# Expert stage of an attention, mixture and dense kernel: place of one weight split per expert, and the queue of the row loads

## The chip, the cores and the metric

One core of a Trainium2 chip runs the whole kernel. The metric is the device time of one execution in microseconds; it is the median of several runs.

## What is computed

Three stages follow each other, each fed by the one before: attention within clusters, a mixture of 8 experts, and a dense network with 2048 hidden columns. The change lies in the mixture. Its reference:

```python
e_idx = np.argmax(x @ w_gate, axis=1)
for e in range(E):                      # E = 8, x is 1536 x 512
    mask = e_idx == e
    h = np.maximum(x[mask] @ w1[e], 0.0)        # w1[e]: 512 x 1024
    ye = h @ w2[e]                              # w2[e]: 1024 x 512
    out[mask] = gate_w[mask, None] * eom[mask, e, None] * ye
```

The products are made in fp32 precision out of two rounded parts each: a value is split into a high part (rounded by a cast) and a low part (the value less the high part), and the product sums high x high, high x low and low x high.

## The kernel before, in words

The routing stage sorts the token rows by expert into a buffer in memory (`xd`) and writes a small table (`plan`) that says which expert comes first (experts are worked off by falling number of rows, with 320, 272, 240, 224, 208, 192, 176 and 160 columns, the table `CAPS`) and where its rows lie. Below, expert 0 is the one that is worked off first, expert 7 the last.

The expert stage is one loop (L1054 to L1088) over groups g = 8e + c, eight for an expert (c0 to c7), each over 128 of the 1024 hidden columns. The program is written in the order in which every engine is to work (a manual schedule), so the order of the emitted lines is each engine's order. One group emits:

- `split_pair` of the weight half that is needed three groups later: ACT casts 128x1024 fp32 values from the buffer `raw` to the high half (L750), and the low half is a subtraction (L753), on POOL in three groups of four, and on DVE, put off to the end of the group, where c is 3 or 7. Then `loads_to` issues the load of the weight half that comes four later into the `raw` buffer that this frees (four buffers, SP's queue, L736). Such an issue waits until the low half has been taken.
- In two or three late groups of an expert, `win_x`: 128 rows of the next expert (`xr`, loaded through `win_load`, L821) are transposed on PE (L834, into `pxt`), and split by ACT (L838) and DVE (L839).
- `win_h`: PE forms the hidden columns (`ph`, L846 to L851). From expert 2 on (at most 256 columns) the two halves of the sum lie side by side in PSUM: ACT copies one (`hs`, L856), DVE adds the other (L857), function `total`. ACT takes relu as the high part (L871, `ht`), and DVE makes the low part (L874), put off to the end of the group.
- `win_y` of the group two earlier: PE adds that group's share to the four sums `py` (L846 to L851). The sums of one expert fill four PSUM buffers, and there is no second set: the next expert's first `win_y` (in its group c2) can start once they have been read.
- In group c1, where the expert before has its last share, `win_out` reads those sums. With at most 256 columns it does so by four `total`s into `room` (ACT L856 and DVE L857 four times); then ACT casts `room` to `yth` (L898), and POOL makes `ytl` (L899), both put off to the end of the group. With more columns (experts 0 and 1, so in group c1 of experts 1 and 2) ACT casts the sums themselves (L902) and DVE makes the low part (L903).
- At the end of the group: the low halves put off, then one step of `dense_step`, which prepares the weights of the dense stage: ACT L784, DVE L785, L788, L791 and L794, ACT L799 and POOL L800, one or two of these in a group.
- In group c0, `win_start(e + 1)` loads the rows of the next expert: one DMA for all of them, into the one `xr` buffer, on SP's queue, behind the weight load of that group.

The register values that such a DMA needs (the expert's place, `exps`) are read from `plan` by SP ahead of the loop.

```python
            if g + 3 < len(order):
                n_, half = order[g + 3]
                split_low = split_pair(ekeys[n_], half, None, nc.vector if g % 4 == 3 else nc.gpsimd, g % 4 == 3)
                loads_to(g + 7)
```

Of the kernel before, what the change touches and what calls it, by code (L numbers as in the profile page):

```python
# [21 lines left out]
NT = B * S  # L22
DM = H * D
E = 8
# [4 lines left out]
CAPS = (320, 272, 240, 224, 208, 192, 176, 160)  # L29
# [6 lines left out]
ACT_E, DVE_E, POOL_E, SP_E = mybir.EngineType.Activation, mybir.EngineType.DVE, mybir.EngineType.Pool, mybir.EngineType.SP  # L36
# [9 lines left out]
def attention_moe_ffn(ctx: ExitStack, tc: tile.TileContext, q, k, v, centroids, w_gate, w_og, w1, w2, w_in, w_out, out):  # L46
    nc = tc.nc
    const = ctx.enter_context(tc.tile_pool(name="const", reuse_waits="tile", bufs=1))

    def f32(ap):  # L50
        return ap.bitcast(F32)
# [37 lines left out]
    xd = dram.tile([E * NT, DM], F32, name="xd")  # L89
# [545 lines left out]
    pieces = {}  # L635
# [8 lines left out]
    with tc.manual_schedule():  # L644
# [14 lines left out]
        for i in range(NS + 2):  # L659
            nu, r = divmod(i + 3, 12)  # L660
# [22 lines left out]
            n = i - (1 if tail else 2)  # L683
# [25 lines left out]
    def need(x, names):  # L709
        for nm in names:  # L710
            tc.add_manual_dep(x, nm, DATA_DEP, reason="all of them scattered")

    def experts(ap):
        return nc.values_load_multi_w_load_instructions(ap, engines=[SP_E], min_val=0, max_val=E - 1)[1]

    exps = list(experts(lead))

    ps_y = ctx.enter_context(tc.tile_pool(name="ps_y", reuse_waits="tile", bufs=1, space=PSUM))
# [9 lines left out]
    def load_half(key, i, ex, pool=None):  # L728
        d = pairs.setdefault(key, {})
        if ex is None:  # L730
            src = pair_of(w_in, w_out, key[2])
        else:
            src = pair_of(w1[bass.ds(ex, 1)].rearrange("o d f -> (o d) f"), w2[bass.ds(ex, 1)].rearrange("o f d -> (o f) d"), key[2])
        t = (pool or raw).tile([128, 1024], F32, name="raw", tag="raw")
        g = src[i].shape[1]
        nc.sync.dma_start(out=t.rearrange("p (g n) -> p g n", g=g), in_=src[i])  # L736
        d["raw", i] = t

    def halves(d, half, pool=None):

        if ("w", half) not in d:
            d["w", half] = (pool or wp).tile([128, 2, 1024], F32R, name=f"w{half}", tag=f"w{half}")
        return d["w", half]

    def split_pair(key, half, pool=None, eng=None, defer=False):
        d = pairs[key]
        w = halves(d, half, pool)
        r = d.pop(("raw", half))
        hi, lo = w[:, 0], w[:, 1]
        nc.scalar.copy(hi, r)  # L750

        def rest():
            (eng or nc.gpsimd).tensor_tensor(lo, r, f32(hi), op=ALU.subtract)  # L753
        if defer:
            return rest
        rest()
# [51 lines left out]
        return pairs[key]["w", 1][:, part].rearrange("p (i d) -> p i d", i=2)[:, i]  # L808


    def win_load(ex_row, n, one_tile=False, pieces=False):
        nr = -(-n // 128)
        if one_tile:
            x = hp.tile([128, 2 * CAP], F32R, name="ht", tag="ht")[:, None, :DM].bitcast(F32)
        else:
            x = xp.tile([128, WR, DM], F32, name="xr", tag="xr", bufs=1)
        d = {"n": n, "nr": nr, "x": x}
        for r0 in range(0, nr, 1 if pieces else nr):
            m, p = (1, min(128, n - r0 * 128)) if pieces else (nr, 128)
            row = nc.s_assert_within(ex_row + r0 * 128, 0, E * NT - 128, skip_runtime_bounds_check_because="inside the rows of an expert") if r0 else ex_row  # L820
            x = nc.sync.dma_start(out=d["x"][:p, r0:r0 + m], in_=xd[bass.ds(row, m * p)].rearrange("(r p) c -> p r c", p=p)).ins  # L821
            need(x, scatters)
        return d

# [28 lines left out]
    def total(ps, n, t):  # L853

        half = hp.tile([128, max(CAPS[2:])], F32, name="hs", tag="hs", bufs=2)[:, :n]
        nc.scalar.copy(half, ps[:, n:2 * n])  # L856
        nc.vector.tensor_tensor(t, ps[:, :n], half, op=ALU.add)  # L857
        return t
# [28 lines left out]
    def win_out(d, col, defer=False):  # L887
        n = d["n"]
        cs = bass.ds(col, n)
        if n > 256:  # L890
            ys = [py[:, :n] for py in d["py"]]
        else:
            room = xp.tile([128, 4 * max(CAPS[2:])], F32, name="room", tag="room", bufs=1)[:, :4 * n].rearrange("p (m n) -> p m n", m=4)
            ys = [total(d["py"][m], n, room[:, m]) for m in range(4)]

        def rest():
            if n <= 256:
                nc.scalar.copy(yth[:, :, cs], room)  # L898
                nc.gpsimd.tensor_tensor(ytl[:, :, cs], room, f32(yth)[:, :, cs], op=ALU.subtract)  # L899
                return  # L900
            for m, y in enumerate(ys):
                nc.scalar.copy(yth[:, m, cs], y)  # L902
                nc.vector.tensor_tensor(ytl[:, m, cs], y, f32(yth)[:, m, cs], op=ALU.subtract)  # L903
        if defer and n <= 256:
            return rest
        rest()
# [3 lines left out]
    ekeys = [("e", e, c) for e in range(E) for c in range(4)]  # L910
# [3 lines left out]
    order = [(0, 0), (1, 0), (0, 1)]  # L914
# [3 lines left out]
    def loads_to(n):  # L918

        while loaded[0] < min(n, len(order)):  # L920
            n_, half = order[loaded[0]]
            load_half(ekeys[n_], half, exps[ekeys[n_][1]], rawd if loaded[0] < 2 else None)
            loaded[0] += 1
# [4 lines left out]
    wins = {}  # L928

    def win_start(e, pieces=False):  # L930
        wins[e] = win_load(nc.s_assert_within(exps[e] * NT, 0, (E - 1) * NT, skip_runtime_bounds_check_because="a row of experts"), CAPS[e], False, pieces)


    with tc.manual_schedule():
# [3 lines left out]
        for n in range(2):  # L938
            n_, half = order[n]
# [4 lines left out]
    with tc.tile_pool(name="ovp", reuse_waits="tile", bufs=1) as ovp:  # L944
        cnt = ovp.tile([1, 1], F32, name="cnt")
        nc.vector.memset(cnt, 0.0)
        with tc.For_i(0, trips):
# [26 lines left out]
            d = win_load(orow, 128, True)  # L974
# [16 lines left out]
    def dense_load(n):  # L991
        while dl["load"] < min(n, len(units)):
            c, g = units[dl["load"]]
            if wide:
                load_wide(c, g)
            else:
                load_half(("d", 0, c), g, None, rawd)
            dl["load"] += 1
# [36 lines left out]
    with tc.manual_schedule():  # L1035
        loads_to(6)

        z = ps_h.tile([128, 512], F32, name="ph", tag="ph")

        def warm(n):  # L1040
            for m in range(n):
                nc.tensor.matmul(z[:, :128], identb, identb, start=True, stop=True)
        warm(4)
        for r in range(wins[0]["nr"]):
            win_x(wins[0], r)
            if r == wins[0]["nr"] - 1:
                warm(6)
        n_, half = order[2]
        split_pair(ekeys[n_], half)
        loads_to(7)  # L1050
        dense_load(2)
        G = E * 8
        hq = deque()
        for g in range(G + 2):  # L1054
            e, c = divmod(g, 8)
            nxt = wins.get(e + 1)
            r = c - (7 - nxt["nr"]) if nxt else 0
            split_low = low = out_low = None
            if g + 3 < len(order):
                n_, half = order[g + 3]  # L1060
                split_low = split_pair(ekeys[n_], half, None, nc.vector if g % 4 == 3 else nc.gpsimd, g % 4 == 3)
                loads_to(g + 7)
            if nxt and 0 <= r < nxt["nr"]:
                win_x(nxt, r)
            if g < G:
                ht, low = win_h(wins[e], ("e", e, c // 2), c % 2, True)
                hq.append((g, ht))
            if g == G + 1:
                dense_in(0)
            if g >= 2:  # L1070
                g0, ht = hq.popleft()
                e0, c0 = divmod(g0, 8)
                win_y(wins[e0], ("e", e0, c0 // 2), c0 % 2, ht, c0 == 0, c0 == 7)
                if c0 == 7:

                    col = e0 and nc.s_assert_within(offs[e0], LEAST + (e0 - 1) * ((NT - LEAST) // (E - 1)), NT, skip_runtime_bounds_check_because="a sum of counts")
                    out_low = win_out(wins[e0], col, True)
            if split_low:
                split_low()
            for f in (low, out_low):  # L1080
                if f:
                    f()
            dense_step(min(5 * e + max(0, c - 2), 40) + 3 * min(max(0, g - 61), 2))
            if g < G:
                if c == 0 and e + 1 < E:
                    win_start(e + 1)
                if g == 2:
                    offs = nc.values_load_multi_w_load_instructions(plan[:, E:], engines=[ACT_E, DVE_E, POOL_E], min_val=0, max_val=NT)[1]  # L1088
# [45 lines left out]
    with tc.manual_schedule():  # L1134
        gq = deque()
        for g in range(len(seq) + 2):
# [6 lines left out]
            if g >= 2:  # L1143

                for m in range(4) if g < len(seq) or g == len(seq) + 1 else ():
                    for g0, gh, gl in list(gq)[:1] if g < len(seq) else gq:
                        fh, tb, c, i = seq[g0]
# [11 lines left out]
            if g == 2 + B * T:  # L1159
                x = nc.sync.dma_start(out=idxc, in_=idd.rearrange("(t p) o -> p (t o)", p=128)).ins  # L1160
# [34 lines left out]
```

## Time and profile before

| | |
|---|---|
| median of 3 runs | 774.23 us (773.53 to 775.23) |
| the profiled execution | 772.91 us |
| its span in the profile | 771.2 us (so 1.7 us lie around it) |
| PE busy | 732.2 us (95%) |
| DVE, ACT, POOL busy | 516.8, 427.5, 265.3 us (67, 55, 34%) |
| mean granted clock of PE | 0.986 |

Shares are of the span. The attention and the routing take the first 303 us or so, the experts the time from there to about 498 us, the dense network the rest. Times in the rows below are microseconds from the start of the span. "Idle before" in a row is how long its engine had nothing to do before it, with what ended that.

### The profile page before, as it was taken

The page shows a single profiled execution, that of the slowest core. Times are in us where ns is not written, and L with a number is a line of the kernel's source. Part 1 is how long each engine was busy: PE and PEld are TensorE (multiplying, and loading weights), DVE is VectorE, ACT ScalarE, POOL GpSimd, SP SyncE. Part 2 cuts the span into 40 slices and gives each one's busy share as a digit, 9 for nine tenths or more (in the row PEclk, how much of TensorE's full clock was granted, in tenths as well). Part 3 has the DMA queues.
Part 4 walks back from the last instruction along what each step waited for, and adds up shares of the span by engine and source line. Part 5 has one row for each costly group of instructions (what it writes and reads, how often), then busy time and mean ns, then how long its engine had stood idle before and what let it go on. Part 6 is the DMA issues. An engine that isn't in the chain of part 4 may idle for free.

```text
span 771.2 us, 12271 instructions
## 1 busy us (share of the span) xinstructions
PE 732.2 (95%) x4328; PEld 647.8 (84%) x4330; DVE 516.8 (67%) x999; ACT 427.5 (55%) x880; POOL 265.3 (34%) x194
## 2 busy tenths in 40 slices
PE   8999999999999986999999998999999999999996
PEld 5898989899898963999989988877888888888885
DVE  5998898989989884444766667697655567332422
ACT  3786776768677852555767766544534335222221
POOL 4302021020552012766677888444521121120101
PEclk8999999999999996999999999999999999999999
DMA  8874938426260005956566676135531121010101
GB/s 233 183 186 130 263 123 236 134 63 170 64 179 11 1 21 204 309 201 224 200 205 233 233 272 220 54 69 111 82 69 56 54 82 55 0 55 0 55 1 54
DMA packets 65344, 98.23 MB, mean 127 GB/s; under 512 B 8800, under 2 KB 43616, under 8 KB 65280
## 3 DMA queue, kind: packets, MB, share of 16 engines
q1 hardware_dynamic: 62976, 91.12, 40.9%
q0 software_dynamic: 2304, 6.30, 2.2%
q8 instruction: 35, 0.57, 0.3%
q14 instruction: 29, 0.24, 0.1%
HBM read 64.46 MB, written 12.59 MB: 100 GB/s over the span
## 4 chain that ended last, share of the span: by engine, by line
PE 26%; issue 16%; DVE 8%; ACT 4%; POOL 3%; DMA 2%; SPq 0%; POOLq 0%; ACTq 0%; DVEq 0%
PE py L1119 3%; PE ph L1031 3%; PE ph L1030 3%; PE ph L1032 3%; PE py L1118 3%; PE py L1117 3%; ACT w L750 2%; DVE w L753 1%; DVE ph L857 1%; PE ph L850 1%; DVE ct L788 1%; POOL out_dram L1127 1%; PE py L850 1%; PE py L848 1%; DMA xr<-xd 1%
## 5 line engine op out<-in xcount | busy, mean ns | idle before, releaser
L753 POOL TENSOR_TENSOR w<-raw,w 128x1024 fp32r<-128x1024 f32 x47 | 117.6, 2516 | 37.6 <-ACT w L750 20.8
L404 DVE TENSOR_TENSOR ptl<-pt,pth 128x384 fp32r<-128x384 f32 x192 | 98.1, 549 | 22.4 <-ACT pth L403 21.2
L403 ACT CAST pth<-pt 128x384 fp32r<-128x384 f32 x192 | 83.4, 483 | 45.2 <-PE pt L399 45.1
L1102 DVE TENSOR_TENSOR sg<-ph,sg 128x512 f32<-128x512 f32 x48 | 33.2, 691 | 102.8 <-ACT sg L1101 97.3
L391 ACT ACTIVATE P<-sp,nm 128x768 f32<-128x768 f32 x96 | 88.0, 917 | 11.8 <-DVE nm L385 11.8
L385 DVE TENSOR_REDUCE nm<-sp 128x1 f32<-128x768 f32 x96 | 90.8, 947 | 1.9 <-PE sp L383 1.9
L800 POOL TENSOR_TENSOR w<-csq,w 128x512 fp32r<-128x512 f32 x32 | 43.5, 1359 | 136.9 <-ACT w L799 136.9
L1101 ACT ACTIVATE sg<-ph 128x512 f32<-128x512 f32 x48 | 28.7, 598 | 108.2 <-PE ph L1032 107.5
L399 PE MATMUL pt<-ident,P 128*128 128x128 f32 x576 | 81.4, 275 | 1.4 <-DVE ptl L404 1.2
L1119 PE MATMUL py<-w,gl 128*128 128x512 f32 x192 | 75.3, 392 | 2.5 <-DVE gl L1108 2.5
L1031 PE MATMUL ph<-ytl,w 128*128 128x512 f32 x192 | 76.1, 396 | 0.0
L1030 PE MATMUL ph<-yth,w 128*128 128x512 f32 x192 | 75.9, 395 | 0.0
L1032 PE MATMUL ph<-yth,w 128*128 128x512 f32 x192 | 75.5, 393 | 0.0
L399 PEld LDWEIGHTS pt<-ident,P 128*128 128x128 f32 x576 | 67.5, 141 | 9.3 <-DVE ptl L404 5.8
L1118 PE MATMUL py<-w,gh 128*128 128x512 f32 x192 | 75.3, 392 | 0.0
L1117 PE MATMUL py<-w,gh 128*128 128x512 f32 x192 | 74.9, 390 | 0.0
L750 ACT CAST w<-raw 128x1024 fp32r<-128x1024 f32 x64 | 66.8, 1044 | 12.2 <-DMA raw<-in_moe_w_dram 7.2
L382 PE MATMUL sp<-X,Q 128*128 128x384 f32 x192 | 72.9, 380 | 0.4 <-ACT P L391 0.4
L421 PE MATMUL po<-pth,vst 128*128 128x384 f32 x192 | 71.3, 372 | 0.0
L850 PE MATMUL py<-ht,w 128*128 128x480 f32 (+5 forms) x192 | 61.2, 352 | 6.8 <-DVE room L857 4.6
L383 PE MATMUL sp<-Z,Q 80*128 80x384 f32 x192 | 65.4, 340 | 0.5 <-DMA Z<-Hk 0.5
L422 PE MATMUL po<-ptl,vst 128*128 128x384 f32 x192 | 64.7, 337 | 0.0
(221 smaller groups left out, 1731.4 us busy)
## 6 DMA issues: line engine op xcount, KB each, us to landing
raw<-in_moe_w_dram SPq DMA_DIRECT2D x64, 512.0 KB, 3.5
raw<-in_moe_w_in_dram SPq DMA_DIRECT2D x16, 512.0 KB, 3.6
raw<-in_moe_w_out_dram SPq DMA_DIRECT2D x16, 512.0 KB, 3.7
Q<-Hq SPq DMA_DIRECT2D x32, 192.0 KB, 4.0
xd<-zrow SPq DMA_DIRECT2D x8, 768.0 KB, 5.7
ld_q<-in_q_dram SPq DMA_DIRECT2D x8, 384.0 KB, 3.3
ld_k<-in_k_dram SPq DMA_DIRECT2D x8, 384.0 KB, 3.8
ld_v<-in_v_dram SPq DMA_DIRECT2D x8, 384.0 KB, 4.7
```

The costliest lines, as they stand in the source:

```text
L385: nc.vector.tensor_reduce(nm, sp[:, :, :384], op=ALU.max, axis=AX.XY, negate=True)
L391: nc.scalar.activation(P, L["sp"][:, :, :384], AF.Exp, bias=L["nm"], accum_out=L["sm"][:, j % 3:j % 3 + 1])
L399: nc.tensor.transpose(pt[:, r * 128:(r + 1) * 128], L["P"][:, n, r * 128:(r + 1) * 128], ident)
L403: nc.scalar.copy(hi, src)
L404: nc.vector.tensor_tensor(L["ptl"][:, 3 * n:3 * n + 3, qs], src, f32(hi), op=ALU.subtract)
L753: (eng or nc.gpsimd).tensor_tensor(lo, r, f32(hi), op=ALU.subtract)
L1030: nc.tensor.matmul(ph, wa(key, 0, k, i), yth[:, k, cs], start=(k == 0), stop=False)
L1031: nc.tensor.matmul(ph, wa(key, 0, k, i), ytl[:, k, cs], start=False, stop=False)
L1032: nc.tensor.matmul(ph, wa(key, 1, k, i), yth[:, k, cs], start=False, stop=(k == 3))
L1117: nc.tensor.matmul(po[m], gh[:, ms], wb(key, 0, i), start=first, stop=False)
L1118: nc.tensor.matmul(po[m], gh[:, ms], wb(key, 1, i), start=False, stop=False)
L1119: nc.tensor.matmul(po[m], gl[:, ms], wb(key, 0, i), start=False, stop=last)
```

## The change

Two things. The split of group c1 of experts 1 to 7 (ACT's cast, POOL's low half and the load behind them) is emitted after `win_out`, so behind ACT's reads of the finished sums, where it stood ahead of `win_h`. And the loads of the rows of experts 1 to 7 are issued by ACT; the register values are therefore read by ACT too (a further small read of `plan` on ACT ahead of the loop). The change adds six lines, so lines behind L1056 have other numbers after it.

```diff
--- before.py
+++ after.py
@@ -711,7 +711,7 @@
             tc.add_manual_dep(x, nm, DATA_DEP, reason="all of them scattered")
 
     def experts(ap):
-        return nc.values_load_multi_w_load_instructions(ap, engines=[SP_E], min_val=0, max_val=E - 1)[1]
+        return nc.values_load_multi_w_load_instructions(ap, engines=[SP_E, ACT_E], min_val=0, max_val=E - 1)[1]
 
     exps = list(experts(lead))
 
@@ -808,7 +808,7 @@
         return pairs[key]["w", 1][:, part].rearrange("p (i d) -> p i d", i=2)[:, i]
 
 
-    def win_load(ex_row, n, one_tile=False, pieces=False):
+    def win_load(ex_row, n, one_tile=False, pieces=False, queue=nc.sync):
         nr = -(-n // 128)
         if one_tile:
             x = hp.tile([128, 2 * CAP], F32R, name="ht", tag="ht")[:, None, :DM].bitcast(F32)
@@ -818,7 +818,7 @@
         for r0 in range(0, nr, 1 if pieces else nr):
             m, p = (1, min(128, n - r0 * 128)) if pieces else (nr, 128)
             row = nc.s_assert_within(ex_row + r0 * 128, 0, E * NT - 128, skip_runtime_bounds_check_because="inside the rows of an expert") if r0 else ex_row
-            x = nc.sync.dma_start(out=d["x"][:p, r0:r0 + m], in_=xd[bass.ds(row, m * p)].rearrange("(r p) c -> p r c", p=p)).ins
+            x = queue.dma_start(out=d["x"][:p, r0:r0 + m], in_=xd[bass.ds(row, m * p)].rearrange("(r p) c -> p r c", p=p)).ins
             need(x, scatters)
         return d
 
@@ -928,7 +928,7 @@
     wins = {}
 
     def win_start(e, pieces=False):
-        wins[e] = win_load(nc.s_assert_within(exps[e] * NT, 0, (E - 1) * NT, skip_runtime_bounds_check_because="a row of experts"), CAPS[e], False, pieces)
+        wins[e] = win_load(nc.s_assert_within(exps[e] * NT, 0, (E - 1) * NT, skip_runtime_bounds_check_because="a row of experts"), CAPS[e], False, pieces, nc.scalar if e else nc.sync)
 
 
     with tc.manual_schedule():
@@ -1056,10 +1056,14 @@
             nxt = wins.get(e + 1)
             r = c - (7 - nxt["nr"]) if nxt else 0
             split_low = low = out_low = None
-            if g + 3 < len(order):
+
+            def split():
                 n_, half = order[g + 3]
-                split_low = split_pair(ekeys[n_], half, None, nc.vector if g % 4 == 3 else nc.gpsimd, g % 4 == 3)
                 loads_to(g + 7)
+                return split_pair(ekeys[n_], half, None, nc.vector if g % 4 == 3 else nc.gpsimd, g % 4 == 3)
+
+            if g + 3 < len(order) and not (c == 1 and e):
+                split_low = split()
             if nxt and 0 <= r < nxt["nr"]:
                 win_x(nxt, r)
             if g < G:
@@ -1075,6 +1079,8 @@
 
                     col = e0 and nc.s_assert_within(offs[e0], LEAST + (e0 - 1) * ((NT - LEAST) // (E - 1)), NT, skip_runtime_bounds_check_because="a sum of counts")
                     out_low = win_out(wins[e0], col, True)
+            if g + 3 < len(order) and c == 1 and e:
+                split_low = split()
             if split_low:
                 split_low()
             for f in (low, out_low):
```

ACT in groups c0 and c1 of expert 6 (`py` are the sums of expert 5; the first row is the relu of c0), before:

```order
L871 ACTIVATE ht<-ph 128x176
L750 CAST w_6472<-raw 128x1024
L856 COPY hs<-ph 128x176
L871 ACTIVATE ht<-ph 128x176
L856 COPY hs<-py_6263 128x192
L856 COPY hs<-py_6264 128x192
L856 COPY hs<-py_6265 128x192
L856 COPY hs<-py_6266 128x192
L898 ISA
L898 COPY yth<-room 128x4x192
L750 CAST w_6515<-raw 128x1024
```

The cast of c1 stands second, ahead of that group's `hs`; it is followed by the four reads of the sums. The same place after the change:

```order
L871 ACTIVATE ht<-ph 128x176
L821 ISA
L821 DMA xr<-xd 128x2x512
L856 COPY hs<-ph 128x176
L871 ACTIVATE ht<-ph 128x176
L856 COPY hs<-py_6265 128x192
L856 COPY hs<-py_6266 128x192
L856 COPY hs<-py_6267 128x192
L856 COPY hs<-py_6268 128x192
L750 CAST w_6511<-raw 128x1024
L898 ISA
L898 COPY yth<-room 128x4x192
```

Where the cast stood there is now the issue of a DMA, and the cast stands behind the four reads and ahead of the cast of `room`. The ISA row is the set-up of a register for the row behind it. DVE's and POOL's order stays as it was.

SP in group c0 of expert 0, between the weight loads (L736) and two loads for the dense stage (L764), before:

```order
L736 ISA
L736 DMA raw<-in_moe_w_dram 128x2x512
L764 DMA raw<-in_moe_w_in_dram 128x2x512 x2
L821 ISA
L821 DMA xr<-xd 128x3x512
L736 ISA
L736 DMA raw<-in_moe_w_dram 128x4x256
```

The load of the rows for expert 1 is fourth and fifth, in front of the next weight load. The same place after the change:

```order
L736 ISA
L736 DMA raw<-in_moe_w_dram 128x2x512
L764 DMA raw<-in_moe_w_in_dram 128x2x512 x2
L736 ISA
L736 DMA raw<-in_moe_w_dram 128x4x256
```

Both rows are gone from SP, and SP goes from the loads for the dense stage to the next weight load. ACT at that place, where the cast of c1 keeps its place since expert 0 has no expert before it, after the change:

```order
L871 ACTIVATE ht<-ph 128x320
L821 ISA
L821 DMA xr<-xd 128x3x512
L750 CAST w_4723<-raw 128x1024
L871 ACTIVATE ht<-ph 128x320
L750 CAST w_4744<-raw 128x1024
```

The DMA stands between the relu of c0 and the cast of c1.

## Rows read from the trace of the kernel before

**Rows 1.** Busy us by stretch: PE, PEld, DVE, ACT, POOL; then granted clock, DMA share, GB/s.

```profile
306.00:334.00 28.00, 26.43 (x174) 25.61 (x174) 12.28 (x18) 13.95 (x22) 17.56 (x7) 0.94 0.85 288
334.00:360.00 26.00, 26.00 (x205) 26.00 (x204) 12.34 (x20) 14.62 (x24) 16.00 (x7) 1.00 0.59 197
452.00:470.00 18.00, 16.55 (x116) 15.61 (x115) 11.55 (x25) 12.92 (x28) 14.65 (x7) 1.00 0.71 247
```

**Rows 2.** Waits view from 306 to 480: total us, times, longest.

```profile
PE py L850 <- DVE room L857: 4.6, 4, 1.4
PE ph L850 <- DVE ht L874: 1.3, 1, 1.3
```

**Rows 3.** Timeline of PE: start, us, engine, line, operation, tiles [idle before, releaser].

```profile
320.44 0.66 PE L834 MATMUL pxt<-ident,xr 128*128 128x128 f32 x4 [1.57 <-DMA xr<-xd]
...
458.06 0.43 PE L850 MATMUL py<-ht,w 128*128 128x352 f32 x1 [1.36 <-DVE room L857]
...
465.53 0.32 PE L850 MATMUL py<-ht,w 128*128 128x352 f32 x1
```

**Rows 4.** SP queue and ACT at expert 0; the load line by source; its landing.

```profile
311.19 0.43 ACT L871 ACTIVATE ht<-ph 128x320 fp32r<-128x320 f32 x1
...
312.86 0.38 SPq L821 DMA_DIRECT2D xr<-xd  x1
...
L821 SPq DMA_DIRECT2D xr<-xd x10: 346/373/587, 298.7 to 454.5; - x10
DMA to landing us min/median/max: 2.6/5.4/7.5
...
raw<-in_moe_w_dram SPq DMA_DIRECT2D x64, 512.0 KB, 3.5
```

**Rows 5.** Timeline of ACT where expert 5 ends, in expert 6.

```profile
455.35 1.04 ACT L750 CAST w<-raw 128x1024 fp32r<-128x1024 f32 x1
457.23 0.54 ACT L856 COPY hs<-py 128x192 f32<-128x192 f32 x2
458.09 0.58 ACT L856 COPY hs<-py 128x192 f32<-128x192 f32 x2 [0.33 <-DVE room L857]
459.10 0.84 ACT L898 CAST yth<-room 128x768 f32 x1 [0.42 <-DVE room L857]
...
465.89 0.32 ACT L871 ACTIVATE ht<-ph 128x176 fp32r<-128x176 f32 x1 [0.48 <-DVE ph L857]
466.10 1.04 ACT L750 CAST w<-raw 128x1024 fp32r<-128x1024 f32 x1
```

**Rows 6.** Timeline of POOL in the same stretch.

```profile
457.27 2.39 POOL L753 TENSOR_TENSOR w<-raw,w 128x1024 fp32r<-128x1024 f32 x1
460.01 1.55 POOL L899 TENSOR_TENSOR ytl<-room,yth 128x768 f32 x1 [0.35 <-ACT yth L898]
461.52 2.40 POOL L753 TENSOR_TENSOR w<-raw,w 128x1024 fp32r<-128x1024 f32 x1
465.28 2.57 POOL L753 TENSOR_TENSOR w<-raw,w 128x1024 fp32r<-128x1024 f32 x1 [1.36 <-ACT w L750]
```

**Rows 7.** Timeline of DVE in the same stretch, and one later row.

```profile
463.25 1.76 DVE L753 TENSOR_TENSOR w<-raw,w 128x1024 fp32r<-128x1024 f32 x1
464.93 0.33 DVE L874 SCALAR_TENSOR_TENSOR ht<-ph,ht 128x176 fp32r<-128x176 f32 x1
465.19 0.41 DVE L785 TENSOR_SCALAR ct<-raw 128x512 int32<-128x512 int32 x1
...
466.50 1.91 DVE L788 SCALAR_TENSOR_TENSOR ct<-raw,ct 128x512 int32<-128x512 int32 x1
...
474.20 1.21 DVE L753 TENSOR_TENSOR w<-raw,w 128x1024 fp32r<-128x1024 f32 x1
```

**Rows 8.** The same operation in expert 7, and grouped over the stage.

```profile
486.71 2.51 DVE L785 TENSOR_SCALAR ct<-raw 128x512 int32<-128x512 int32 x1
...
L785 DVE TENSOR_SCALAR ct<-raw 128x512 int32<-128x512 int32 x10 | 8.2, 816 | 0.1
```

## The prediction

> **What bounds the kernel now.** I read the busy times by stretch first. While experts 0 and 1 run, PE is all but full: 26.43 of 28.0 us at a granted clock of 0.94, then 26.00 of 26.0 at 1.00 [rows 1]. By expert 6 it is not: 16.55 of 18.0, at the same clock of 1.00, with POOL at 14.65 [rows 1]. So early experts are paid for in PE time, later ones by what PE waits for. The waits view names that: 4.6 us, in four waits, for DVE's additions into `room`, which set the sums' PSUM buffers free for the next expert, and 1.3 us, once, for the low part of a hidden tile [rows 2]. PE's timeline puts one `room` wait at 458.06, 1.36 us, in expert 6, and shows one more wait, 1.57 us at 320.44, for the rows of expert 1 [rows 3]. Both halves of the change aim at these waits: at most 1.57 and 4.6 us are there to be had.
>
> The engine timelines tell whether they can be had. In expert 6 PE takes the tile of c3 at 465.53 [rows 3], and DVE had finished it at 464.93 + 0.33 = 465.26 [rows 7]: 0.27 us of margin. A delay of the chain ACT, DVE, POOL by more than a few tenths therefore stops PE.
>
> **A fact about DVE and POOL that the sum needs.** L785 takes 0.41 us in expert 6 [rows 7] and 2.51 in expert 7 [rows 8]; the ten of the stage have a mean of 0.816 [rows 8], so a few are long. DVE's low half L753 takes 1.21 us at 474.20 and 1.76 at 463.25 [rows 7]. In the long case POOL was subtracting: its low half from 461.52 ends at 463.92 [rows 6], and L753 ends at 465.01, 1.09 us behind that, about its own length. At 465.19 L785 came 0.09 us ahead of POOL's low half of 465.28, and that one then took 2.57 us instead of 2.40 [rows 6]. So these DVE operations (both inputs, or one wide input, in SBUF) and POOL's subtractions run one after the other, whoever is second waiting for the whole of the other. L788 at 466.50 waited for that one's end, 467.85, and got its turn then, though the cast for POOL's next low half had ended at 467.14 (466.10 + 1.04 [rows 5]): it ends at 466.50 + 1.91 = 468.41 [rows 7]. A waiting DVE goes before POOL's next operation.
>
> **The change part by part.**
>
> 1. *Register values on ACT.* A small load of `plan` ahead of the loop. The loop begins when SP is through its own reads and DMAs (the last one at 298.68 and later), and ACT has nothing else there. I take 0; without that cover it costs the few tenths of a us that such a read waits.
>
> 2. *Rows of expert 1.* SP issued them at 312.86, behind a weight load and two loads for the dense stage; ACT will after its relu of 311.19, at about 311.5 [rows 4]. PE's wait is 1.57 us [rows 3]. Landing takes 2.6 to 7.5 us, 5.4 in the median [rows 4]; issued 1.35 us earlier and with less ahead of it, the transfer should be in by 318.8. Bounds: nothing, if the engines serve the same bytes in the same order of time, and 1.57, the wait. I take 1.57, nearer to the median landing. PE is full afterwards [rows 1], so this gain is kept: **-1.6**. The waits view lists no wait for the rows of experts 2 to 7, so these gain nothing.
>
> 3. *ACT's part of group c1.* A cast of 1.04 us (the next operation starts 0.95 after it) leaves the place ahead of `hs` [rows 5]; in experts 1 to 6 the issue of a DMA comes there. ACT's price for that is in no row; SP's is 0.35 to 0.59 [rows 4], and with its register rows I take 0.58, between nothing and the 0.95 that would undo the gain. So the reads of the sums start 0.95 - 0.58 = 0.37 us earlier, and 0.95 in expert 7, which loads no rows. That shortens the four `room` waits by at most 3 x 0.37 + 0.95 = 2.1 us. Whether it stays depends on the next item.
>
> 4. *POOL's low half of c1.* Today it starts at 457.27 [rows 6]. Now the cast stands behind the four reads, which end at 458.67 - 0.37 = 458.3 (458.09 + 0.58 in [rows 5]); it ends at 459.25, and POOL can start at 459.3. Its three operations in a row, 2.40 + 1.55 + 2.40 [rows 6], which today end at 463.92, now end at 465.65. The cast of `room` stands 0.42 us idle today [rows 5], and goes into the time after the moved cast with about no delay (459.15 for 459.10), so ACT's next groups start as today. The collision is on DVE. L753 of c3 asks at 463.25 as before; POOL's `ytl` ends at 461.7 + 1.55 = 463.27. If DVE goes first, L753 ends at 464.4, POOL's low half of c2 takes 464.4 to 466.85, and L785, which asks at 464.8, waits for that: as in expert 7, where POOL ended at about 488.9 and L785 at 489.22 [rows 8], it ends 0.3 us behind, at 467.15 and not 465.60. Behind it stands the sum of group c4 and its relu, at 467.4 for 465.89 [rows 5]: 1.5 us late. POOL's low half of c4 is next, to about 469.5, and L788 ends 0.56 behind it as it did (468.41 - 467.85), at 470.1 for 468.41. From there the order holds both engines some 1.65 us late to the end of the expert; PE's margins of a few tenths take off little, and I have **+1.6** for an expert, the gain of item 3 already in it, since it is worked from ACT's new times. Experts 4, 5 and 6 have this form: L785 just ahead of POOL there, as the mean of ten in [rows 8] has room for two long ones only, 0.41 x 8 + 2 x 2.4 = 8.1 of 8.2. So **3 x 1.6 = +4.8**. The ends: -0.37 in each (the delay is absorbed) and +3.9 (below).
>
> 5. *Experts 3 and 7.* These hold the two long L785; the collision is there already, and PE's 1.3 us in expert 3 [rows 2] is its price. POOL comes some 0.6 us later in both; I take **+0.5 each**, between -0.95 (the earlier sums of expert 7 kept whole) and +1.6.
>
> 6. *Experts 1 and 2.* The cast moves behind four L902, no `room` is waited for, and PE is full; POOL has 16.0 busy in 26.0 us [rows 1]. 0, covered by POOL's idle time; without it up to +1.6.
>
> 7. *Weight loads.* The `raw` buffer of c1 is free at 461.7 and not at 459.66; the next load of it lands 3.5 us later [rows 4], at 465.3, ahead of its cast at 466.10 [rows 5]: 0. SP loses seven issues and waits anyway for buffers: 0.
>
> The sum is -1.6 + 4.8 + 1.0 = **+4.2 us**. Against the profiled execution, 772.9 (a span of 771.2 and 1.7 around it), that is 777.1; that execution lies 1.3 us under the median of the runs, so for the median I say 774.23 + 4.2 = **778.4 us**.
>
> **Rivals.**
>
> - *The sums come free earlier and nothing pushes back* (faster). For it: the `room` wait is the largest on PE, POOL has idle time (1.36 us before 465.28 [rows 6]), and DVE's low half may be late without PE noticing. Against it: the margin of 0.27 us. Price: -1.6 - 2.1 = -3.7, so 770.5. The point: POOL's low half of c4, ready at 465.28 [rows 6], must not stand ready when L753 ends, so L753 must end by 465.2, POOL's c2 by 464.1 and the cast by 457.8; I have 459.25. Or the gaps of DVE and POOL later in the expert give the time back before PE asks. Chance 0.20.
> - *Gains and losses cancel*: one or two of the three experts collide, the others keep 0.37. With one, -1.6 + 1.6 - 0.7 + 0 to 1 = about 0; with two, about +2. 773.5 to 775.7. Chance 0.17.
> - *POOL first.* L753 asks at 463.25 and `ytl` ends at 463.27: a tie. If POOL's low half of c2 gets in first, L753 waits until 465.67, ends at 466.8, POOL's low half of c4 takes the next 2.40 us, and L785 ends near 469.5: 3.9 us late, not 1.6. One expert of this kind gives 778.4 + 2.3 = 780.7, all three 785.3. In L788's row the waiting DVE won [rows 7], but it had waited for 1.35 us. Chance 0.13. The Trainium skill has a rule for this tie (SBUF — State Buffer, "Who interferes with whom"): whichever of the two engines issues first holds the shared ports for the whole instruction. By that, a POOL operation that follows straight on `ytl` would be first wherever DVE asks even a little after its end; by the same rule L788, which asked while POOL was busy, came before POOL's next, and here the trace agrees.
> - *The rows land no earlier*, the change doing there only what it says in the program: +5.8, so 780.0. Against it: three loads stood ahead on one queue [rows 4]. Chance 0.08, within slower.
>
> **How the numbers follow.** My forecast has 0.42. A difference of 0.2% (1.5 us) is about what a measurement of this kernel can tell from no change. Faster by more than that is the first rival, 0.20; same is the second, 0.17; slower is the rest, 0.42 + 0.13 + 0.08 = 0.63. The range reaches from 771.0, most of the first rival, to 782.5, between one and two experts of the third kind.
>
> **What would show it.** The wait of 1.57 us for the rows of expert 1 should be gone, and `room` waits in experts 4 to 6 shorter by some 0.4 us each. If I am right, L785 takes over 2 us in experts 4, 5 and 6 too, POOL's low half of c1 starts 2 us later, and PE gains waits for the hidden tiles' low parts (L874) from c3 on. I am wrong if the mean of L785 stays near 0.8, or if those waits appear without the time getting longer.

## The result and the profile after

| | before | after |
|---|---|---|
| median | 774.64 us (773.53 to 775.23, 5 runs) | 780.21 us (779.05 to 783.16, 5 runs) |
| profiled execution, its span | 772.91, 771.2 | 782.47, 780.8 |
| mean granted clock | 0.986 | 0.976 |

The change makes the kernel slower by 5.6 us: ratio 1.0081, 95% interval 1.0061 to 1.0102, that is 4.7 to 7.9 us. The profiled execution of after lies 2.3 us over its median and that of before 1.7 us under its own, so the two traces differ by more than the medians do; the five executions of after had mean clocks of 0.976 to 0.985, and the two longest had the two lowest.

The waits view of the kernel after, 306 to 505, PE's waits in the expert stage (total us, times, longest):

```profile
PE ph L850 <- DVE ht L874: 5.3, 4, 1.5
PE py L850 <- DVE ht L874: 5.2, 6, 1.7
PE py L850 <- DVE room L857: 1.2, 2, 0.8
```

The waits for the sums' additions (`room`) have shrunk from 4.6 us [rows 2] to 1.2, and no wait for the rows of expert 1 (1.57 us [rows 3]) is left. The waits for the low parts of hidden tiles have grown to 10.5 us in ten. Before, 1.3 of these stood in [rows 2] and, up to the end of the stage at 498, this row of the same view:

```profile
PE py L850 <- DVE ht L874: 2.1, 3, 1.0
```

So hidden tiles cost 7.1 us more (10.5 - 1.3 - 2.1), and the sums 3.4 less. Where the new waits come from stands on three engine timelines of expert 6. POOL:

```profile
466.04 2.41 POOL L753 TENSOR_TENSOR w<-raw,w 128x1024 fp32r<-128x1024 f32 x1 [2.19 <-ACT w L750]
468.40 1.55 POOL L899 TENSOR_TENSOR ytl<-room,yth 128x768 f32 x1
469.91 5.72 POOL L753 TENSOR_TENSOR w<-raw,w 128x1024 fp32r<-128x1024 f32 x2
```

Its low half of c1 starts after an idle 2.19 us that ends with ACT's cast, and the three operations then follow each other without a gap (the first three of [rows 6] had one gap, of 0.35 us). DVE:

```profile
470.01 3.40 DVE L753 TENSOR_TENSOR w<-raw,w 128x1024 fp32r<-128x1024 f32 x1
473.33 0.33 DVE L874 SCALAR_TENSOR_TENSOR ht<-ph,ht 128x176 fp32r<-128x176 f32 x1
473.58 2.34 DVE L785 TENSOR_SCALAR ct<-raw 128x512 int32<-128x512 int32 x1
```

L753 stands ready at 470.01, when POOL's low half of c2 has been under way for 0.10 us (469.91), and takes 3.40 us in place of 1.76 [rows 7]: it waits for the whole of it. POOL's low half of c4, the second of the pair of 5.72 us, goes next, and L785 takes 2.34 us in place of 0.41. ACT, which made the moved cast at 464.91 behind the reads of the sums:

```profile
464.43 0.58 ACT L856 COPY hs<-py 128x192 f32<-128x192 f32 x2 [0.33 <-DVE room L857]
464.91 1.05 ACT L750 CAST w<-raw 128x1024 fp32r<-128x1024 f32 x1
465.86 0.84 ACT L898 CAST yth<-room 128x768 f32 x1
...
476.20 0.32 ACT L871 ACTIVATE ht<-ph 128x176 fp32r<-128x176 f32 x1 [4.04 <-DVE ph L857]
```

The last row is the relu of group c4. It comes 6.19 us after the start of L753 (476.20 - 470.01), where it came 2.64 after it before (465.89 [rows 5] less 463.25 [rows 7]): 3.55 us late. PE feels it twice: in the sums that take the tile of c3, and in the product that forms the next hidden columns (`ph`), which waits until DVE has made the low part of c4:

```profile
473.71 0.43 PE L850 MATMUL py<-ht,w 128*128 128x352 f32 x1 [1.68 <-DVE ht L874]
...
476.95 0.66 PE L850 MATMUL ph<-t,w 128*128 128x352 f32 x1 [1.49 <-DVE ht L874]
```

The same pair of waits stands in experts 4 and 5. The ten L785 of the stage, 8.2 us before [rows 8]:

```profile
L785 DVE TENSOR_SCALAR ct<-raw 128x512 int32<-128x512 int32 x10 | 17.5, 1746 | 0.1
```

**The times by expert.** PE's first product with the hidden tile of c2 starts, for experts 3 to 7, at 395.63, 419.29, 441.25, 462.86 and 484.12 before, and at 397.07, 420.67, 444.93, 469.19 and 492.82 after. From one to the next that is 23.66, 21.96, 21.61 and 21.26 us before, and 23.60, 24.26, 24.26 and 23.63 after: 0.1 less for expert 3, and 2.3, 2.65 and 2.4 us more for experts 4, 5 and 6. L785 is long in experts 1 and 2 as well (2.23 and 2.30 us after, 0.42 before), but there the time from c2 to c2 is 23.75 us before and after for expert 1, and 21.9 and 22.3 for expert 2.

**The clock falls too.** The busy time by stretch of the kernel after (PE, PEld, DVE, ACT, POOL, then granted clock, DMA share, GB/s):

```profile
440.00:445.00 5.00, 5.00 (x33) 4.77 (x34) 1.76 (x6) 4.57 (x8) 3.44 (x2) 1.00 0.58 207
445.00:450.00 5.00, 3.54 (x25) 3.28 (x24) 4.62 (x4) 2.41 (x6) 5.00 (x3) 1.00 0.46 159
450.00:455.00 5.00, 3.54 (x20) 3.22 (x19) 3.74 (x7) 2.35 (x6) 3.06 (x2) 0.81 0.86 261
455.00:460.00 5.00, 5.00 (x32) 5.00 (x31) 4.59 (x8) 3.64 (x9) 2.99 (x2) 0.85 0.39 126
...
470.00:475.00 5.00, 3.32 (x24) 2.92 (x22) 5.00 (x4) 2.03 (x4) 5.00 (x2) 1.00 0.51 181
475.00:480.00 5.00, 3.51 (x17) 3.37 (x17) 3.76 (x8) 2.99 (x6) 3.00 (x2) 0.70 0.67 227
480.00:485.00 5.00, 5.00 (x37) 5.00 (x36) 4.53 (x8) 3.51 (x9) 2.97 (x2) 0.96 0.51 172
```

PE is full at a clock of 1.00 until the two waits come, is busy 3.54 and 3.32 of 5 us with the first, and the stretch behind has 0.81 in expert 5 and 0.70 in expert 6: PE ran for part of it at 1.2 GHz in place of 2.4. Before, expert 6 had 1.00 [rows 1]. If all of that were PE's time, 5 x (0.19 + 0.15 + 0.30 + 0.04) = 3.4 us were lost. With the waits' 7.1 - 3.4 = 3.7 us this makes 7.1 of the 8.5 us by which the stage of the experts (measured below) is longer in these two traces. What makes the clock fall stays open: not every stretch with idle time does it, as one of the kernel before shows, in which PE is busy 2.96 of 5 us:

```profile
475.00:480.00 5.00, 2.96 (x20) 2.68 (x20) 2.35 (x8) 3.90 (x11) 4.78 (x3) 1.00 0.84 305
```

The loads of the rows, now on ACT's queue, landed sooner, the slowest in 5.3 us, where it was 7.5 [rows 4]:

```profile
L821 ACTq DMA_DIRECT2D xr<-xd x7: 379/380/446, 312.9 to 461.8; - x7
...
DMA to landing us min/median/max: 2.7/4.4/5.3
```

### The profile page after: what moved, and what is told of

Read it like the earlier page. It is cut to its first block, busy times and chain, and to the rows that moved or that the text cites. A ratio compares the mean times of both kernels' runs of the same rounds, so it can differ in the third digit from the quotient of the medians.

```text
span 780.8 us, 12274 instructions
## 1 busy us (share of the span) xinstructions
PE 739.2 (95%) x4328; PEld 653.9 (84%) x4330; DVE 528.1 (68%) x999; ACT 426.9 (55%) x880; POOL 268.9 (34%) x194
## 5 line engine op out<-in xcount | busy, mean ns | idle before, releaser
L753 POOL TENSOR_TENSOR w<-raw,w 128x1024 fp32r<-128x1024 f32 x47 | 121.5, 2599 | 48.8 <-ACT w L750 29.1
L404 DVE TENSOR_TENSOR ptl<-pt,pth 128x384 fp32r<-128x384 f32 x192 | 98.2, 549 | 22.3 <-ACT pth L403 20.7
L850 PE MATMUL py<-ht,w 128*128 128x480 f32 (+5 forms) x192 | 62.8, 359 | 6.5 <-DVE ht L874 5.2
L850 PE MATMUL ph<-t,w 128*128 128x480 f32 (+5 forms) x192 | 62.3, 357 | 5.4 <-DVE ht L874 5.3
```

Of the source, the lines that this page charges most:

```text
L404: nc.vector.tensor_tensor(L["ptl"][:, 3 * n:3 * n + 3, qs], src, f32(hi), op=ALU.subtract)
L850: nc.tensor.matmul(ps[:, :2 * n], w_hi, t, start=first, stop=False)
```

## The experiments

Theory A is the prediction's: the low half that comes late on POOL collides with DVE's L753 and L785. Theory B lays the loss to the change of queue, theory C to the cast's later place on ACT itself.

Each kernel was run 5 to 12 times, beside runs of the kernel before. The medians of before move between the sets (774.6 to 776.1), so each run is compared with its own. A second measure comes from the traces, one for each kernel: the time from PE's first product with the hidden tile of expert 1's group c2 to ACT's last relu of expert 7, "stage" below. It leaves out the attention, the routing and the load of expert 1's rows, which vary from execution to execution. Before it was 495.65 - 349.97 = 145.7 us, after 505.20 - 351.02 = 154.2.

| kernel | median, us | its before | ratio (95%) | stage, us |
|---|---|---|---|---|
| split alone | 784.59 | 775.71 | 1.0114 (1.0092 to 1.0136) | 153.3 |
| queue alone | 774.49 | 775.71 | 0.9981 (0.9962 to 0.9999) | 146.7 |
| rows of expert 1 alone | 773.00 | 775.71 | 0.9963 (0.9948 to 0.9978) | 145.7 |
| POOL late alone | 783.42 | 775.71 | 1.0096 (1.0074 to 1.0118) | 153.2 |
| after, c1 on DVE | 778.06 | 775.59 | 1.0044 (1.0031 to 1.0058) | 150.9 |
| rows of expert 1, c1 on DVE | 776.81 | 775.59 | 1.0016 (1.0002 to 1.0029) | 149.8 |
| the same, c5 too | 788.01 | 775.59 | 1.0164 (1.0142 to 1.0186) | 160.1 |
| rows of expert 1, L785 first | 769.64 | 776.14 | 0.9923 (0.9907 to 0.9938) | 142.6 |
| after, L785 first | 786.74 | 776.14 | 1.0138 (1.0117 to 1.0160) | 159.7 |
| after, c1 on DVE, L785 first | 769.84 | 776.14 | 0.9934 (0.9912 to 0.9956) | 143.2 |
| rows of expert 1, c1 on DVE, L785 first | 770.99 | 776.14 | 0.9945 (0.9926 to 0.9964) | 143.7 |
| the same with the late cast | 769.97 | 775.37 | 0.9934 (0.9915 to 0.9953) | 142.3 |

**1. The split alone** (the change without its two lines on the queue; here and below `...` stands for code left out).

```diff
-... engines=[SP_E, ACT_E] ...
+... engines=[SP_E] ...
-... CAPS[e], False, pieces, nc.scalar if e else nc.sync)
+... CAPS[e], False, pieces)
```

> The kernel before with the split of group c1 emitted behind the sums, rows still loaded on SP's queue. Theory A (the late low half of c1 on POOL runs into DVE's L753 and L785 in experts 4 to 6): slower than before by 6 to 8 us, 781 to 783, since the 1.57 us of PE's wait for the rows of expert 1 stay; L785 takes some 17 us in ten runs, as in the changed kernel, where it took 8.2 before. Theory B (the change of queue costs the time, by ACT's issues and a later start of the loop): 774 to 775.5, L785 near 8.

8.9 us slower, somewhat more than the 6 to 8 that I expected, and the stage takes 7.6 us more. Theory B falls. The experts' first product does come later in the trace of the changed kernel, 17.75 us behind the routing's last (`pnt`, L581) for 16.91 before, but it is as late here (17.77), where ACT reads no register values. The waits of PE from 306 to 505, and L785:

```profile
PE py L850 <- DVE ht L874: 5.3, 6, 1.7
PE ph L850 <- DVE ht L874: 5.2, 4, 1.5
...
PE py L850 <- DVE room L857: 0.5, 1, 0.5
```
```profile
L785 DVE TENSOR_SCALAR ct<-raw 128x512 int32<-128x512 int32 x10 | 17.5, 1745 | 0.1
```

The rows of the hidden tiles and L785 are those of the changed kernel, to a tenth; `room` has 0.5 us for 1.2. The whole of the loss comes from the place of the split.

**2. The queue alone** (the kernel before with the two lines on the queue).

> The kernel before with the rows of experts 1 to 7 loaded through ACT's queue, split where it was. Theory A: faster by 0.5 to 1.5 us, 773.1 to 774.1: PE's 1.57 us wait for the rows of expert 1 goes, and the issue of a DMA, some 0.58 us, stands ahead of ACT's reads of the sums in experts 2 to 6 and gives up to 0.5 us of it back; L785 near 8 us. Theory B: slower by 2 us or more, 776.6 to 780, with the loop's first matmul some 0.8 us later against the end of the plan, as it was in the profile of the changed kernel.

1.2 us faster, by an interval that just leaves out no change. The waits for `room` are longer than the 4.6 us of [rows 2]:

```profile
PE py L850 <- DVE room L857: 5.7, 4, 1.7
```

1.1 us over the three experts 4 to 6 is 0.37 us for an issue on ACT, and the stage is 1.0 us longer. ACT in group c0 and c1 of expert 6 (ACTq is the part of the engine that issues):

```profile
456.79 0.32 ACT L871 ACTIVATE ht<-ph 128x176 fp32r<-128x176 f32 x1 [0.42 <-DVE ph L857]
456.94 0.38 ACTq L821 DMA_DIRECT2D xr<-xd  x1
457.36 1.06 ACT L750 CAST w<-raw 128x1024 fp32r<-128x1024 f32 x1 [0.26 <-issue]
```

The issue takes 0.38 us while the relu still runs, and the cast behind it waits 0.26 us. Theory A holds, with a price of some 0.37 us for an issue where I had 0.58.

**3. The rows of expert 1 alone on ACT's queue** (against run 2).

```diff
-... nc.scalar if e else nc.sync)
+... nc.scalar if e == 1 else nc.sync)
```

> As the run before this one, but the rows of expert 1 alone go through ACT's queue, those of experts 2 to 7 through SP's. Theory A: faster than before by 1.2 to 1.6 us, 773.0 to 773.4, and not slower than with all seven on ACT. Theory B (the register values that ACT reads ahead of the loop delay its start): not faster than before, 774.6 or more.

2.7 us faster, 1.7 to 4.0 by the interval, where I expected 1.2 to 1.6: more than the 1.57 us of PE's wait, at the stage's old length of 145.7. That wait isn't the same in every execution. With the rows on SP's queue it was 0.47 us in the trace of run 1 and 3.13 in that of run 4:

```profile
322.53 0.33 PE L834 MATMUL pxt<-ident,xr 128*128 128x128 f32 x1 [0.47 <-DMA xr<-xd]
```
```profile
324.36 0.48 PE L834 MATMUL pxt<-ident,xr 128*128 128x128 f32 x1 [3.13 <-DMA xr<-xd]
```

So 1.57 was one value out of a spread that 2.7 lies in; how long it was in the timed executions of the kernel before no trace shows.

**4. POOL late alone.** In group c1 of experts 3 to 7 the low half is put off behind the old sums' low part, on POOL alone.

```diff
-... half, None, nc.vector if g % 4 == 3 else nc.gpsimd, g % 4 == 3)
+... half, None, nc.vector if g % 4 == 3 else nc.gpsimd, g % 4 == 3 or (c == 1 and e >= 3))
...
+            late = c == 1 and e >= 3
-            if split_low:
+            if split_low and not late:
...
-            for f in (low, out_low):
+            for f in (low, out_low, late and split_low):
```

> The kernel before, where in experts 3 to 7 only POOL's order in group c1 is turned: the low part of the old expert's sums (L899) first, then the low half of c1's weights. ACT's and DVE's order, the cast and the queues are as before. Theory A (POOL's lateness alone is the cost): POOL's low half of c2 ends some 2 us later, as in the changed kernel, L785 takes 15 us or more in ten runs, and the time is 778 to 784. Theory C (the cost comes from the cast's place on ACT): 774 to 775.5, L785 near 8.

7.7 us slower with ACT as before: theory C falls, and a late POOL is enough. In expert 6, POOL's `ytl` first, then four low halves in a row, and DVE's L785 blocked among them:

```profile
470.00 1.55 POOL L899 TENSOR_TENSOR ytl<-room,yth 128x768 f32 x1 [2.63 <-ACT yth L898]
471.51 11.06 POOL L753 TENSOR_TENSOR w<-raw,w 128x1024 fp32r<-128x1024 f32 x4
```
```profile
475.15 2.36 DVE L785 TENSOR_SCALAR ct<-raw 128x512 int32<-128x512 int32 x1
```

But the loss is not made in quite the same way: DVE's L753 keeps its turn there (1.74 us in expert 6), L785 alone loses in experts 4 to 6, and PE also waits for the low half of c1 itself, 4.2 us, as here no time is left for it. The waits for `room` stay, though PE is late here too:

```profile
PE py L850 <- DVE room L857: 5.2, 4, 1.3
PE py L851 <- POOL w L753: 4.2, 5, 1.1
```

**5. The changed kernel with c1's low half on DVE** at the end of the group, in experts 3 to 7 (`late` as in 4, and `nc.vector if g % 4 == 3 or late`).

> The changed kernel, with the low half of group c1's weights in experts 3 to 7 made by DVE at the end of that group instead of by POOL. Theory A (the late low half on POOL is the cost): POOL's next low half starts as early as before, L785 in ten runs falls from 17 us to under 9, and most of the 5.6 us comes back: 770 to 775. Theory C (the cast's later place on ACT costs by itself): still 778 or more, with L785 short.

2.5 us slower than its own before, where the changed kernel was 5.6: some 3 us come back, a little over half and not the most of it that I expected. Theory C's time (778 or more) came, but not with a short L785, so it isn't shown either; it falls in run 10. L785 is as long as ever, which I had not expected; run 6 shows why:

```profile
L785 DVE TENSOR_SCALAR ct<-raw 128x512 int32<-128x512 int32 x10 | 17.9, 1787 | 0.1
```

**6. The same in the kernel before, with the rows of expert 1.**

> The kernel before with the rows of expert 1 on ACT's queue, the split where it was, and the low half of group c1 in experts 3 to 7 on DVE at the end of the group. If the shared access of DVE and POOL to SBUF is what limits late experts (POOL's low half holds it 2.40 us, DVE's 1.1 to 1.2), 1.2 us an expert are saved in 3 to 7: 767 to 771 for 773.0 with the rows of expert 1 alone. If PE or ACT limits them: 772.5 to 773.5.

3.8 us slower than the rows of expert 1 alone: the shared access as a sum of busy times is not the limit. Expert 6 shows why. DVE's new low half in c1 makes POOL's `ytl` wait (1.84 us for 1.55 [rows 6]), and some tenths later POOL's low half of c4 comes in ahead of L785:

```profile
460.68 1.84 POOL L899 TENSOR_TENSOR ytl<-room,yth 128x768 f32 x1 [2.68 <-ACT yth L898]
...
465.94 2.37 POOL L753 TENSOR_TENSOR w<-raw,w 128x1024 fp32r<-128x1024 f32 x1 [1.06 <-ACT w L750]
```
```profile
466.14 2.46 DVE L785 TENSOR_SCALAR ct<-raw 128x512 int32<-128x512 int32 x1
```

465.94 and 466.14, where it was 465.28 and 465.19 before [rows 6, 7]. L785 then takes 2.46 us. That race of 0.1 us, won by DVE in experts 4 to 6 of the kernel before, is what I take to decide; runs 8 and 11 take it away.

**7. c5's low half on DVE too** (`late = c in (1, 5) and e >= 3`).

> As the run before, with the low half of group c5 on DVE too (half of the low halves of experts 3 to 7 on each engine). If the shared access limits: another 0.5 to 3 us less, 765 to 770. If DVE becomes the limit (the sums of a group then wait behind its low halves): slower than the run before, by up to 3 us.

11.2 us slower than run 6, outside both of my expectations. Now the step of group c5, L791, loses the race as well (its mean was 0.91 us in run 6):

```profile
L791 DVE SCALAR_TENSOR_TENSOR ct<-raw,ct 128x512 int32<-128x512 int32 x8 | 15.8, 1981 | 0.0
```

**8. L785 ahead of L753 in group c3**, with the rows of expert 1 on ACT's queue. ACT, POOL and SP have the same order as in run 3.

```diff
+            if c == 3:
+                dense_step(min(5 * e + max(0, c - 2), 40) + 3 * min(max(0, g - 61), 2))
             if split_low:
                 split_low()
...
-            dense_step(min(5 * e + max(0, c - 2), 40) + 3 * min(max(0, g - 61), 2))
+            if c != 3:
+                dense_step(min(5 * e + max(0, c - 2), 40) + 3 * min(max(0, g - 61), 2))
```

> The kernel before with the rows of expert 1 on ACT's queue, and in group c3 of each expert DVE's L785 ahead of its low half L753 instead of behind the hidden tile's low part. Theory A, sharpened (what costs is L785 losing against POOL's low half of c4, 2.1 us for DVE each time): no L785 waits for the c4 half any more; it can wait 0.7 us for the c2 half, which L753 did before. PE's waits in experts 3 and 7 (1.34, 0.42 and 0.97 us) go, the hidden tile of c3 comes 0.3 us later in experts 4 to 6 (0.1 us of PE each): 770.5 to 772 for 773.0. Theory D (a late hidden tile of c3 costs as much): 773 or more.

6.5 us faster than before, better than expected, and 3.4 us under run 3. By the times from c2 to c2, 2.4 of the stage's 3.1 us are won in experts 3 and 7 (1.3 and 1.1), the two in which L785 lost before. In expert 6 L785 waits the half us that POOL's c2 still needs, and L753, with all fifteen of its kind, waits for nothing:

```profile
460.38 0.95 DVE L785 TENSOR_SCALAR ct<-raw 128x512 int32<-128x512 int32 x1
461.26 1.21 DVE L753 TENSOR_TENSOR w<-raw,w 128x1024 fp32r<-128x1024 f32 x1
```
```profile
L753 DVE TENSOR_TENSOR w<-raw,w 128x1024 fp32r<-128x1024 f32 x15 | 18.2, 1213 | 0.0
```

PE's waits for `room` are as before; those for the hidden tiles have gone from 3.4 us (1.3 and 2.1) to 1.1:

```profile
PE py L850 <- DVE room L857: 4.5, 4, 1.4
PE py L850 <- DVE ht L874: 1.1, 2, 0.8
```

**9. The changed kernel with L785 first.**

> The changed kernel with L785 ahead of L753 in group c3, nothing else. There POOL's low half of c2 wins the tie at that place, so L785 waits the 2.4 us that L753 waited, and L753 then stands against POOL's c4 half: by theory A one lost race takes the place of another, 778 to 782, with L753 on DVE long (over 2.5 us) and L785 long too. If the place of L785 alone decided: 770 to 773.

Slower still, 786.7, outside what I expected: L785 now waits for POOL's c2, L753 behind it for POOL's c4, and both stand ahead of the hidden tile of c3, so PE waits up to 4.2 us at one place (306 to 520):

```profile
L753 DVE TENSOR_TENSOR w<-raw,w 128x1024 fp32r<-128x1024 f32 x15 | 31.2, 2080 | 0.0
```
```profile
PE py L850 <- DVE ht L874: 16.2, 5, 4.2
```

**10. The changed kernel with c1 on DVE and L785 first.**

> The changed kernel with c1's low half on DVE in experts 3 to 7 and L785 ahead of L753 in c3: POOL's order is early again and L785 out of its way. Theory A: both lost races gone, 769 to 773, faster than before although the cast stands where the change put it; L785 below 1.2 us in the mean. Theory C (the cast's place on ACT costs by itself): 776 or more.

769.84: the changed kernel's cast stays where the change put it, and with both lost races gone in experts 3 to 7 it is 6.3 us faster than before, as fast as run 8. Theory C falls here too. (In expert 1, where the low half of c1 stays on POOL, one L753 still takes 3.44 us, and the time from c2 to c2 stays 23.75.)

```profile
PE py L850 <- DVE ht L874: 3.6, 6, 1.5
PE py L850 <- DVE room L857: 1.9, 4, 0.8
```

**11. The kernel before with the same two steps, and the rows of expert 1.**

> The kernel before with the rows of expert 1 on ACT's queue, c1's low half on DVE in experts 3 to 7, and L785 ahead of L753 in c3. Theory A: 769 to 772, about as the run with the late cast and not above the first run of this set by more than 1 us; if DVE's extra low half costs what it did in the earlier run without the turn of L785 (3.8 us over the rows of expert 1 alone), 775 or more.

770.99. The low half on DVE brings nothing on its own: run 8 has 769.64 without it, 1.35 us less. But that is all it costs now that L785 is out of the way, where it was 3.8 between runs 3 and 6.

```profile
PE py L850 <- DVE room L857: 4.5, 4, 1.4
PE py L850 <- DVE ht L874: 1.6, 3, 1.1
```

**12. The same with the cast behind the sums:** the first part of the change, freed of what it collides with.

> The kernel of the run before this (rows of expert 1 on ACT's queue, c1's low half on DVE in experts 3 to 7, L785 ahead of L753), with the cast of c1 behind the sums as the change has it: the first part of the change with the collisions taken away. Theory A (the cast's later place is a gain once POOL's lateness is taken away): the waits of PE for the sums' additions shrink by about 0.95 us each, no new wait for a hidden tile; 767.5 to 770 for 771.0. Theory C (no gain in it, the sums were waited for by nobody who sets the end): 770.5 to 772.

769.97, with a ratio to its own before (0.9934) that run 11's (0.9945) does not differ from within the intervals:

```profile
PE py L850 <- DVE ht L874: 3.7, 6, 1.5
PE py L850 <- DVE room L857: 1.1, 2, 0.6
```

Against run 11 the waits for `room` fall by 3.4 us and those for hidden tiles grow by 2.1. What the change was to win at the sums is there, and most of it is handed on to the next wait. Neither theory is shown: the time lies in theory A's range, but with the new waits that A ruled out, and the gain is 1.4 us by the stage of one trace each (143.7 to 142.3) and not clear of noise by the runs.

## Why the prediction was right, point by point

The forecast was slower, 778.4 for 774.23, +4.2 us; measured were 780.21 and +5.6, inside the range of 771.0 to 782.5, and the mechanism is the one of item 4, a late POOL that holds up DVE, though in the third rival's form. The sizes of its terms:

- *Item 2, the rows of expert 1*: -1.6 forecast, PE's wait gone in every trace with the load on ACT, and -2.7 measured (1.7 to 4.0).
- *Item 3, an issue on ACT*: 0.58 us forecast, 0.37 measured.
- *Item 4, the step that was mis-sized.* I let DVE's L753 go first at a tie: it was to ask at 463.25, and POOL's `ytl` to end at 461.7 + 1.55, which is 463.25 and not the 463.27 that I wrote. POOL went first, in expert 6 by 0.10 us, and the same long L753 stands in experts 4 and 5 (3.36 us both). That is the third rival's mechanism, which I gave 0.13. Its delay was nearly as worked out there, 3.55 us for the relu of c4 (3.9 in the rival, 1.5 in my forecast). But an expert became slower by 2.3 to 2.65 us and not by 3.9: 7.3 in the three, where I had 4.8. Part of the difference is the waits for the sums, which gave back 3.4 us where item 3 allowed at most 2.1. Most of that comes from the cast's place: with the cast moved and no lost race in these experts the waits are 1.9 us (run 10), with POOL late and ACT as before 5.2 (run 4).
- *Item 5, experts 3 and 7*: +0.5 each forecast; expert 3 was 0.1 faster, and from c2 of expert 7 to the last relu it is 12.38 us for 11.53, so +0.85.
- *Items 1, 6 and 7, put at nothing*: experts 1 and 2 cost 0.0 and 0.4 us. From 340 to 492 neither trace has a wait of ACT for a weight load, so a late `raw` buffer is not the cause. The register values were no delay either, as run 1 shows.
- *Not in the forecast*: the fall of PE's clock behind the new waits, up to 3.4 us in the profiled execution. So my sum came out near the result in part by luck, with terms too large and too small that nearly made up for each other: over the experts it measures 0.0 + 0.4 - 0.1 + 7.3 + 0.85 = 8.5 us in the traces for my 5.8, and with the 2.7 of the rows taken off 5.8 for my 4.2, beside 5.6 measured.

With the parts measured one by one: +8.9 for the split, -1.2 for the queue, together +7.7; both at once +5.6 (4.7 to 7.9). The Trainium skill (SBUF — State Buffer, "Who interferes with whom") gives the ports that the two share to whichever of them issues first, for the whole instruction; the trace agrees (POOL at 469.91, ahead of DVE's 470.01). At my tie it was for neither. I let the row of L788 weigh more, where DVE had asked 1.35 us before POOL could go on.

## What to carry to other kernels

Where two engines exclude each other, a schedule rests on who asks first at a few places, and the time depends on those races more than on any sum of busy times; find them in the timelines of both engines, and order the short operation ahead of the long one rather than rely on a tenth of a us (run 8), but look first at what then stands behind it: with POOL late the same order cost more (run 9). A cast that is moved takes with it the low half behind it on another engine: follow that one to what it blocks next. Before costing a wait that goes, ask what PE waits for next; in run 12, 2.1 of the 3.4 us won at the sums were lost at the hidden tiles.

## What the runs showed of the hardware that I had not expected

- At the end of a POOL subtraction a DVE operation that is already waiting goes before POOL's next one (L788 [rows 7]), but one that asks 0.10 us after POOL's next has started waits until that one, of 2.4 us, is through (L753 of 470.01).
- Behind two waits of PE of about 1.5 us the granted clock was 0.81 in expert 5 and 0.70 in expert 6; behind a like pair in expert 4 (1.28 and 1.43) it stayed at 1.00.
- A DMA issued by ACT costs its next operation only some 0.3 to 0.4 us, as the issue of 0.38 us lies beside the operation that still runs.
